# Loading and sorting the second batch's values later in a fused attention and mixture kernel

## The chip, the cores and the metric

The kernel runs on one core of one Trainium2 chip. The metric is the device time of one execution in microseconds (us), as the median of several runs; lower is better. The profile is one execution taken by the hardware profiler. Its engines are PE (TensorE matmul; PEld is its weight load), DVE (VectorE), ACT (ScalarE), POOL (GpSimd) and SP (SyncE, which here only issues DMAs).

## The reference

Four batches of eight heads, 768 positions of 64 numbers each. A small 8 x 8 matrix per head (`sort_net`) is normalised five times over rows and columns, and mixes the eight blocks of 96 positions of keys and values ("sorting"). Each block of queries then attends to the sorted block of the same place. The result, 3072 tokens of 512 numbers, goes through a layer of eight experts, whose outputs are weighted by a matrix P that is balanced in eight rounds.

```python
P = sort_net
for _ in range(5):
    P = exp(P - max(P, -1)); P = P / (sum(P, -1) + 1e-9); P = P / (sum(P, -2) + 1e-9)
k_sorted = einsum('bhij,bhjcd->bhicd', P, k_blocks)
v_sorted = einsum('bhij,bhjcd->bhicd', P, v_blocks)
attn = softmax(q_blocks @ k_sorted.T / 8)
x = (attn @ v_sorted).transpose(0, 2, 1, 3).reshape(3072, 512)
...
for e in range(8):
    out += Pm[:, e:e+1] * (maximum(x @ w1[e], 0) @ w2[e])
```

## The kernel before, in words

The kernel has three phases. In the first, the small matrices are normalised on 32 partitions (lines 413 to 431, ACT and DVE in turn, five rounds) while the first batch's queries, values and keys are loaded; then the whole attention of batch 0 runs with two-bank PSUM tiles called `pair`, four of them. In the second, the attention of batches 1 to 3 is woven, step by step, with the first expert's layer for tokens that are ready (`hidden0` computes its hidden units, `output0` its outputs), with eight one-bank PSUM tiles called `bank`. In the third and by far the longest, from about 115 us, the other experts run with sums in the manner of Strassen. The change touches the first phase and the start of the second.

One batch's attention has these steps. Values: `sort_pair` (two heads at once, line 268) or `sort_values` (line 156) multiply the loaded values by R, the expanded matrix of the batch, and copy the product to the tile `vs`, on ACT (for batch 0 half of them on DVE). `hop` (line 148) then moves `vs` by eight DMAs, one for each block ("piece"), into `vsb`, where the 96 positions of a block lie on partitions; there are two such tiles, one for even and one for odd batches. Keys (k0 to k3, two heads each) are multiplied by R likewise; queries (q0 to q3) are transposed, and ACT copies them to `qTs`. Scores (s0 to s3) are matmuls of both, and ACT takes their exponential into `atp`. A mix (m0 to m3: `wide_mix` in batch 0, `mix` after it) multiplies `atp` by `vsb`, and DVE divides by the sums into `og`: a reciprocal (line 337) and a product (line 339) in batch 0. A turn (t0 to t3) transposes `og`, and ACT or DVE copies it to `xtT`, from which `hidden0` reads; kk numbers its four parts, one for each pair of heads. `logits` (l0, l3) feeds the balance.

The order of the work on PE is written out by hand. The helper `pin` keeps a DMA or an instruction in the program's order on its engine, and almost every matmul is pinned. In the second phase `run_both` takes one step of an attention (or of `sort_values`) and then as many steps of the first expert as a list says; a step of `hidden0` is four matmuls and an activation on ACT (line 372), a step of `output0` four matmuls with w2 (line 379). Every engine works through its own list in order, and waits for others by semaphores; what stands behind a waiting instruction waits as well. PSUM tiles are used in turn, so a matmul can also wait until an engine has read the tile's former content.

The loads from HBM are issued by POOL and form one queue: batch 0's q, v and k first, then a small weight, then batch 1's v (line 97). The loads behind these stand behind a gate (line 454), a tiny copy on POOL that reads the first two pieces of batch 0's `vsb`: w1 in two halves, batch 1's k and q, w2, and then batch 2's v, k and q (line 522). Between the pieces of batch 0 and the gate, POOL also builds batch 1's R (line 453). Pieces: batch 0's are issued by SP, POOL and ACT in turn, batch 1's by SP alone, those of batches 2 and 3 by SP and POOL in turn.

`warm` (line 322) issues matmuls of a zero tile whose product nobody reads; it has `Ibig`, the identity that POOL makes, as its weights. Such unread products stand at the start (four), ahead of `spread` (seven; `spread` expands the normalised matrix, line 437), and here and there in batch 0's attention.

In batch 0's attention the first phase also sorts batch 1's values: `sort_pair(1, ...)` stands between its mixes (line 463), with four copies on ACT, and `hop(1)` at its end (line 476).

Of the kernel before, what the change touches and what calls it, by code (L numbers as in the profile page):

```python
# [25 lines left out]
def kernel(  # L26
# [11 lines left out]
    nc = tc.nc  # L38
# [25 lines left out]
    pin = tc.keep_in_program_order  # L64
    kt, vt, qt = {}, {}, {}

    def load_batch(bb, parts):
        for x, l0, n in parts:
            d, src = {"v": (vt, v), "k": (kt, k), "q": (qt, q)}[x]
            if bb not in d:  # L70
                d[bb] = kvp.tile([128, 8, 384], BF16, name="kvq", bufs=5)
            pin(nc.gpsimd.dma_start(
                out=d[bb][:, l0:l0 + n, :],
                in_=src[bb, l0:l0 + n].rearrange("h (p kk) d -> p h (kk d)", kk=6)))

    w1t = {}
# [15 lines left out]
    Ibig = ones.tile([128, 128], BF16)  # L92
# [1 line left out]
    load_batch(0, [(x, l0, 4) for x in "vk" for l0 in (0, 4)])  # L94
    wg = ones.tile([128, 4, E], BF16)
    pin(nc.gpsimd.dma_start(out=wg, in_=moe_w_gate.rearrange("(kk k) e -> k kk e", k=128)))
    load_batch(1, [("v", 0, 8)])
    blank = perp.tile([128, 512], BF16)
    nc.vector.memset(blank, 0.0)
    mask16 = ones.tile([128, 16], F32)  # L100
# [8 lines left out]
    xtT = xtp.tile([128, 4, N], BF16)  # L109
# [21 lines left out]
    def build_r(bb, eng, n, pbps=None):  # L131

        Rt[bb] = perp.tile([128, 8, 8, 16], BF16, name=f"R{bb % 2}")
        for h in range(0, 8, n):
            ins = eng.tensor_tensor(
                out=mkap(Rt[bb], [Rt[bb].ap[0], [16, 8 * n], [1, 16]] if pbps is None else
                         [Rt[bb].ap[0], [128, n], [16, 8], [1, 16]], off=h * 128),
                in0=(mkap(Pb, [Pb.ap[0], [1, 8 * n], [0, 16]], off=(bb * 8 + h) * 8)
                     if pbps is None else
                     mkap(pbps, [pbps.ap[0], [1, n], [32, 8], [0, 16]], off=h)),  # L140
                in1=mkap(mask16, [mask16.ap[0], [0, 8 * n], [1, 16]] if pbps is None else
                         [mask16.ap[0], [0, n], [0, 8], [1, 16]]),
                op=ALU.mult)
            if eng is nc.gpsimd:
                pin(ins)


    def hop(bb):
        for i in range(NB):
            eng = ((nc.sync, nc.gpsimd, nc.scalar)[i % 3] if bb == 0 else  # L150
                   nc.gpsimd if i % 2 and bb > 1 else nc.sync)
            (pin if bb == 0 else lambda ins: ins)(eng.dma_start(
                out=mkap(vsbt[bb % 2], [[VW, 96], [1, 520]], off=i * 520),
                in_=vs[16 * i:16 * i + 16].rearrange("p kk h d -> p kk (h d)")))
# [98 lines left out]
    held = pp.tile([96, 2], BF16)  # L253
# [67 lines left out]

    def warm(t, n):
        for _ in range(n):
            pin(nc.tensor.matmul(t[:, 0, :], Ibig, blank, start=True, stop=True))

    def wide_mix(hp, pair):
        og[0, hp] = sp.tile([128, NB, 2, 64], BF16, name="og", bufs=2)
        for h in range(2):
            t = pair()
            warm(t, h == 0 and hp > 0)  # L330
            for i in range(NB):
                c, a = (i % 4) * 65, (i * 8 + 2 * hp + h) * 65
                pin(nc.tensor.matmul(t[0:96, i // 4, c:c + 65], at[0, hp, h][0:96, i, :],
                                     vsbt[0][0:96, a:a + 65], start=True, stop=True))
            recips = sp.tile([128, NB], F32, name="recips")
            ps = t[0:96, :, 0:260].rearrange("p b (j x) -> p b j x", j=4)
            nc.vector.reciprocal(out=recips[0:96].rearrange("p (b j) -> p b j", b=2),
                                 in_=ps[:, :, :, 64])
            nc.vector.tensor_mul(
                og[0, hp][0:96, :, h, :].rearrange("p (b j) d -> p b j d", b=2),  # L340
                ps[:, :, :, 0:64],
                mkap(recips, [[recips.ap[0][0], 96], [4, 2], [1, 4], [0, 64]]))
# [21 lines left out]
            yield  # L364

    def hidden0(c0, hTs, hbank, fbs=range(8)):
        for fb in fbs:
            hps = hbank()
            for kk in range(4):
                pin(nc.tensor.matmul(hps[:, 0:384], w1t[0][:, kk, fb * 128:(fb + 1) * 128],  # L370
                                     xtT[:, kk, c0:c0 + 384], start=(kk == 0), stop=(kk == 3)))
            nc.scalar.activation(out=hTs[:, fb, 0:384], in_=hps[:, 0:384], func=AF.Relu)  # L372
            yield

# [31 lines left out]
    with tc.tile_pool(name="ps0", bufs=4, space=bass.MemoryType.PSUM,  # L406
                      reuse_waits="tile") as ps0:
        pair = lambda: ps0.tile([128, 2, 512], F32, name="pair")
        warm(pair(), 4)
        rs = pp.tile([32, 8], F32)  # L410
        cs = pp.tile([32, 8], F32)
        Pt = P.rearrange("p i j -> p j i")
        nc.vector.reduce_max(out=rs, in_=P, axis=AX.X)
        nc.vector.tensor_sub(P, P, mkap(rs, [rs.ap[0], rs.ap[1], [0, 8]]))
        for it in range(5):


            pin(nc.scalar.activation(out=P, in_=P, func=AF.Exp))
            for hp in {2: (0, 1), 3: (2,), 4: (3,)}.get(it, ()):
                wide_queries(hp, pair)  # L420
            if it == 1:
                pin(nc.vector.reduce_sum(out=mask16, in_=Ibig.rearrange("p (j c) -> p c j", c=16),
                                         axis=AX.X))
            pin(nc.vector.reduce_sum(out=rs, in_=P, axis=AX.X))
            nc.vector.reciprocal(out=rs, in_=rs)
            nc.vector.tensor_mul(P, P, mkap(rs, [rs.ap[0], rs.ap[1], [0, 8]]))
            nc.vector.reduce_sum(out=cs, in_=Pt, axis=AX.X)
            if it == 0:
                nc.vector.tensor_scalar_add(cs, cs, 1e-9)
            nc.vector.reciprocal(out=cs, in_=cs)  # L430
            nc.vector.tensor_mul(Pt, Pt, mkap(cs, [cs.ap[0], cs.ap[1], [0, 8]]))

        Prep = perp.tile([32, 8, 8, 16], BF16, name="R1")
        for eng, i0, n in ((nc.vector.tensor_copy, 0, 5), (nc.scalar.copy, 5, 3)):
            eng(Prep[:, i0:i0 + n], mkap(P, [P.ap[0], [8, n], [1, 8], [0, 16]], off=i0 * 8))

        def spread(n):
            t = pair()
            warm(t, n)
            pbps = t[:, 0, 0:256].rearrange("p (i g) -> p i g", i=8)  # L440
            for i in range(8):
                pin(nc.tensor.matmul(pbps[:, i, :], Prep[:, i].rearrange("p j c -> p (j c)"),
                                     Ibig[0:32, 0:32], start=True, stop=True))
            return pbps

        build_r(0, nc.vector, 2, spread(7))
        for hp in range(4):
            sort_pair(0, hp, pair)
        wide_keys(0, pair)
        hop(0)  # L450
        wide_keys(1, pair)
        nc.vector.tensor_copy(Pb, spread(0).rearrange("p i g -> p g i"))
        build_r(1, nc.gpsimd, 4)
        gate = nc.gpsimd.tensor_copy(
            held, mkap(vsbt[0], [[VW, 96], [520, 2]], off=519))
        with tc.issue_after(gate.ins):
            load_w1(0, 0, 512)
            load_w1(0, 512, F)
            load_batch(1, [("k", 0, 8), ("q", 0, 4), ("q", 4, 4)])
            load_w2(0)  # L460
        for x in "s0 k2 s1 k3 s2 s3".split():
            (wide_keys if x[0] == "k" else wide_scores)(int(x[1]), pair)
        for x in "v0 v1 m0 v2 m1 t0 v3 m2 t1 m3 t2 t3".split():
            hp = int(x[1])
            if x[0] == "m":
                wide_mix(hp, pair)
            elif x[0] == "v":
                sort_pair(1, hp, pair)
            else:
                if hp == 3:  # L470
                    warm(pair(), 3)
                turn(0, hp, lambda shape, dt: ps0.tile(
                    [128, 2048], dt, name="pair")[:, 0:768].rearrange(
                        "p (i c) -> p i c", i=NB),
                     nc.vector.tensor_copy if hp == 3 else nc.scalar.copy)
        hop(1)

    def weave(a, b, na, nb):

# [7 lines left out]
    with ExitStack() as c2:  # L487
        pa = c2.enter_context(tc.tile_pool(name="pa", bufs=8, space=bass.MemoryType.PSUM,
                                           reuse_waits="tile"))
        bank1 = lambda shape, dt: pa.tile(shape, dt, name="bank", tag="bank")  # L490
# [20 lines left out]
        def run_both(a, counts):  # L511
            for n in counts:
                next(a, 0)
                run(n)
# [3 lines left out]
        run(8)  # L518
        at1 = attention(1, bank1, "k0 k1 k2 q0 q1 s0 q2 s1 k3 q3 s2 "
                                  "m0 s3 m1,t0 m2,t1 m3 t2 t3,l0 l3")  # L520
        run_both(at1, (1, 1, 1, 1, 0, 1, 0, 1, 0, 0, 1))
        load_batch(2, [(x, 0, 8) for x in "vkq"])
        build_r(2, nc.gpsimd, 4)
        run_both(at1, (1, 2, 1, 2))
# [333 lines left out]
```

## Time and profile before

| | |
|---|---|
| median of 3 runs | 678.94 us (677.23 to 679.38) |
| the profiled execution | 677.66 us |
| its span, first to last instruction | 675.6 us |
| PE, DVE, ACT, POOL busy | 659.3, 542.8, 297.4, 469.5 us |
| end of batch 0's attention (first `hidden0` matmul) | 31.70 us |
| batch 1's v load issued, landed | 7.14, 21.21 us |
| batch 0's pieces: first issue, last landing | 16.34, 23.44 us |
| batch 1's pieces: first issue, last landing | 27.82, 39.8 us |
| first mix of batch 1 (m0) on PE | 50.15 us |
| batch 2's pieces: first issue, last landing | 62.87, 69.35 us |

In a row of the timeline stand the start in us, the time it took, the engine (a q behind it: its sequencer, which issues DMAs), the line of the kernel, the operation, the tile written and the tiles read, the shape, and the number of equal instructions merged into the row. In brackets stands how long the engine had been idle before it, and what released it. Times are from the start of the span.

### The profile page before, as it was taken

What the parts mean: (1) busy time and instruction counts of PE and PEld (TensorE: products, weight loads), DVE (VectorE), ACT (ScalarE), POOL (GpSimd) and SP (SyncE); (2) the same over time, 40 slices, a digit from 0 to 9 for tenths busy, and PEclk for the clock granted to TensorE, in tenths of its full rate; (3) what the DMA queues carried; (4) which work ended last, traced back from release to release, by engine and by line L of the source; (5) the groups of instructions that cost most, each with busy time, mean ns of one, the idle gap of its engine ahead of it and who ended that gap; (6) DMA issues with size and microseconds to landing.
All of it is one profiled execution on the core that took longest, in us unless ns stands there. A gap on an engine that the chain in (4) does not pass through costs nothing.

```text
span 675.6 us, 13268 instructions
## 1 busy us (share of the span) xinstructions
PE 659.3 (98%) x5139; PEld 435.2 (64%) x5139; DVE 542.8 (80%) x1133; ACT 297.4 (44%) x536; POOL 469.5 (69%) x494
## 2 busy tenths in 40 slices
PE   6899999999999999999999999999999999999996
PEld 3566675554666666666666666666666666666675
DVE  7528777673798888888898888888898888888896
ACT  4773863479433334333433333333433343333430
POOL 4702435007987998898897998689886999636745
PEclk9999999999999999999999999999999999999999
DMA  9997964002140340031203040034003120001223
GB/s 157 190 216 115 154 114 63 1 0 41 23 64 2 62 64 1 1 64 20 44 1 62 2 64 0 3 62 63 1 1 65 25 39 1 1 0 64 95 79 141
DMA packets 32735, 36.57 MB, mean 54 GB/s; under 512 B 2016, under 2 KB 25792, under 8 KB 32672
## 3 DMA queue, kind: packets, MB, share of 16 engines
q0 software_dynamic: 26672, 27.32, 25.7%
q1 hardware_dynamic: 5776, 8.20, 3.8%
q8 instruction: 40, 0.66, 0.4%
q10 hardware_dynamic: 224, 0.20, 0.1%
q14 instruction: 23, 0.19, 0.1%
HBM read 52.45 MB, written 6.29 MB: 87 GB/s over the span
## 4 chain that ended last, share of the span: by engine, by line
PE 73%; DVE 1%; POOL 1%; issue 0%; ACT 0%; DVEq 0%
PE oacc L715 36%; PE bk L628 35%; PE bk L715 1%; DVE osbl L680 1%; POOL hs L698 1%; DVE hT L664 0%; DVE hT L667 0%; ACT p L648 0%; DVEq L680 0%
## 5 line engine op out<-in xcount | busy, mean ns | idle before, releaser
L680 DVE SCALAR_TENSOR_TENSOR osbl<-oacc,glog,osbl 128x256 f32<-128x256 f32 (+1 forms) x490 | 255.6, 522 | 61.3 <-PE oacc L715 61.2
L628 PE MATMUL bk<-xtT,w1e 128*128 128x512 bf16 x504 | 149.7, 379 | 0.0
L698 POOL TENSOR_TENSOR hs<-hT 128x512 bf16<-128x512 bf16 (+2 forms) x105 | 99.4, 960 | 67.2 <-DVE hT L667 67.1
L715 PEld LDWEIGHTS <-hs 128*128 128x128 bf16 x1008 | 98.5, 98 | 64.6 <-POOL hs L698 1.5
L715 PEld LDWEIGHTS <-hT 128*128 128x128 bf16 x1008 | 98.6, 98 | 64.5 <-issue 1.3
L670 ACT ACTIVATE hT<-bk 128x512 bf16<-128x512 f32 x84 | 50.3, 598 | 158.8 <-PE bk L628 158.8
L715 PE MATMUL oacc<-w2e,hT 128*128 128x256 bf16 x796 | 119.6, 273 | 0.5 <-ACT hT L670 0.5
L698 POOL TENSOR_TENSOR hs<-hT,hs 128x512 bf16<-128x512 bf16 (+2 forms) x105 | 99.9, 959 | 4.9
L698 POOL TENSOR_TENSOR hs<-hs,hT 128x512 bf16<-128x512 bf16 (+2 forms) x105 | 99.9, 960 | 4.3 <-ACT hT L670 0.4
L628 PE MATMUL bk<-xc,wc 128*128 128x512 bf16 x336 | 99.9, 379 | 0.2 <-ACT p L648 0.2
L715 PE MATMUL oacc<-w2e,hs 128*128 128x256 bf16 x612 | 92.0, 273 | 0.9 <-POOL hs L698 0.9
L656 ACT COPY u<-bk 128x512 f32<-128x512 f32 x84 | 49.3, 586 | 95.2 <-PE bk L628 94.5
L628 PEld LDWEIGHTS <-w1e 128*128 128x128 bf16 x672 | 65.7, 98 | 10.5
L664 DVE CUSTOM_DVE_ANT_0 hT<-bk,p 128x512 bf16<-128x512 f32 x84 | 58.1, 692 | 11.8 <-ACT p L661 6.4
L674 DVE SCALAR_TENSOR_TENSOR h<-bk,hT 128x512 bf16<-128x512 f32 x84 | 57.2, 681 | 5.7 <-ACT hT L670 5.7
L661 ACT COPY p<-bk 128x512 f32<-128x512 f32 x84 | 49.3, 586 | 23.5 <-PE bk L628 23.5
L648 ACT COPY p<-bk 128x512 f32<-128x512 f32 x84 | 49.3, 587 | 20.1 <-PE bk L628 20.1
L652 DVE CUSTOM_DVE_ANT_0 hT<-bk,p 128x512 bf16<-128x512 f32 x84 | 57.2, 681 | 1.1 <-ACT hT L372 0.6
L667 DVE CUSTOM_DVE_ANT_0 hT<-bk,u 128x512 bf16<-128x512 f32 x84 | 57.2, 680 | 1.0 <-PE bk L628 1.0
L715 PE MATMUL oacc<-w2s,hs 128*128 128x256 bf16 x364 | 54.8, 273 | 0.1
L628 PEld LDWEIGHTS <-wc 128*128 128x128 bf16 x504 | 49.3, 98 | 8.0 <-issue 0.4
L628 PE MATMUL bk<-xtT,wc 128*128 128x512 bf16 x168 | 50.0, 379 | 0.0
(138 smaller groups left out, 832.3 us busy)
## 6 DMA issues: line engine op xcount, KB each, us to landing
w2e<-in_moe_w_dram POOLq DMA_DIRECT2D x8, 1024.0 KB, 8.9
w1e<-in_moe_w_dram POOLq DMA_DIRECT2D x7, 1024.0 KB, 8.2
out_dram<-osbl SPq DMA_DIRECT2D x23, 256.0 KB, 2.0
kvq<-in_v_dram POOLq DMA_DIRECT2D x3, 768.0 KB, 14.1
kvq<-in_k_dram POOLq DMA_DIRECT2D x3, 768.0 KB, 13.6
vsb<-vs SPq DMA_DIRECT2D x19, 97.5 KB, 5.3
kvq<-in_q_dram POOLq DMA_DIRECT2D x4, 384.0 KB, 10.6
kvq<-in_q_dram POOLq DMA_DIRECT2D x2, 768.0 KB, 21.9
```

Source lines behind the costliest of these rows:

```text
L628: hold(nc.tensor.matmul(ps, wa[:, kk, :], xa[:, kk, :], start=(first and kk == 0), stop=(kk == 1), skip_group_check=True))
L648: nc.scalar.copy(p1, u)
L652: nc.vector._custom_dve(TENSOR_ADD_SAT, out=c11, in0=w, in1=p1, s0=TOP, s1=0.0)
L656: nc.scalar.copy(u2, u)
L661: nc.scalar.copy(p5, v)
L664: nc.vector._custom_dve(TENSOR_ADD_SAT, out=c22, in0=u, in1=p5, s0=TOP, s1=0.0)
L667: nc.vector._custom_dve(TENSOR_ADD_SAT, out=c12, in0=v, in1=u2, s0=TOP, s1=0.0)
L670: nc.scalar.activation(out=c21, in_=u, func=AF.Relu)
L674: nc.vector.scalar_tensor_tensor(out=h3[e, p][:, i, :], in0=u, scalar=0.0, in1=c22, op0=ALU.max, op1=ALU.subtract)
L680: nc.vector.scalar_tensor_tensor(out=o, in0=ps, scalar=glog[:, t, e:e + 1], in1=o, op0=ALU.mult, op1=ALU.add)
L698: nc.gpsimd.tensor_tensor(out=c, in0=a, in1=b, op=o)
L715: nc.tensor.matmul(ps, h[:, fb, :], w[:, fb, :], start=(first and fb == 0), stop=(fb == 3), skip_group_check=True)
```

## The change

Six edits:

1. Batch 1's v load moves from line 97, ahead of the gate, to the list behind the gate, after batch 1's k and q and ahead of w2.
2. The sorting of batch 1's values leaves batch 0's attention. `sort_values(1, ...)` with `hop(1)` at its end now stands in batch 1's attention, after s0 and ahead of q2. The steps of the first expert are shared out anew; their number up to s2 is the same.
3. Batch 0's pieces are issued by SP and POOL in turn, four each, and no longer by ACT. Batch 1's stay with SP alone.
4. `warm` takes its weights from the zero tile itself. There are eleven unread products at the start instead of four, nine ahead of `spread` instead of seven, three new ones ahead of the third group of queries, and one more in the first mix of batch 0.
5. The mixes and turns of batch 0 keep their order without the value products between them.
6. The first steps of `hidden0` hold three PSUM tiles: for hidden blocks 0, 1 and 2 the products of the first three parts of `xtT` are issued ahead of the first product of the fourth part.

```diff
-    load_batch(1, [("v", 0, 8)])
...
-            eng = ((nc.sync, nc.gpsimd, nc.scalar)[i % 3] if bb == 0 else
-                   nc.gpsimd if i % 2 and bb > 1 else nc.sync)
+            eng = nc.gpsimd if i % 2 and bb != 1 else nc.sync
...
-            pin(nc.tensor.matmul(t[:, 0, :], Ibig, blank, start=True, stop=True))
+            pin(nc.tensor.matmul(t[:, 0, :], blank[:, 0:128], blank, start=True, stop=True))
...
-            warm(t, h == 0 and hp > 0)
+            warm(t, h == 0)
...
     def hidden0(c0, hTs, hbank, fbs=range(8)):
+        held = {}
         for fb in fbs:
-            hps = hbank()
-            for kk in range(4):
-                pin(nc.tensor.matmul(hps[:, 0:384], w1t[0][:, kk, fb * 128:(fb + 1) * 128],
-                                     xtT[:, kk, c0:c0 + 384], start=(kk == 0), stop=(kk == 3)))
+            for f, some in (((0, range(3)), (1, range(3)), (2, range(3)), (0, (3,)))
+                            if (c0, fb) == (0, 0) else
+                            ((fb, (3,) if fb in held else range(4)),)):
+                if f not in held:
+                    held[f] = hbank()
+                for kk in some:
+                    pin(nc.tensor.matmul(held[f][:, 0:384],
+                                         w1t[0][:, kk, f * 128:(f + 1) * 128],
+                                         xtT[:, kk, c0:c0 + 384],
+                                         start=(kk == 0), stop=(kk == 3)))
+            hps = held.pop(fb)
...
-        warm(pair(), 4)
+        warm(pair(), 11)
...
+            if it == 3:
+                warm(pair(), 3)
...
-        build_r(0, nc.vector, 2, spread(7))
+        build_r(0, nc.vector, 2, spread(9))
...
-            load_batch(1, [("k", 0, 8), ("q", 0, 4), ("q", 4, 4)])
+            load_batch(1, [("k", 0, 8), ("q", 0, 4), ("q", 4, 4), ("v", 0, 8)])
...
-        for x in "v0 v1 m0 v2 m1 t0 v3 m2 t1 m3 t2 t3".split():
+        for x in "m0 m1 t0 m2 t1 m3 t2 t3".split():
...
-            elif x[0] == "v":
-                sort_pair(1, hp, pair)
...
-        hop(1)
...
-        run_both(at1, (1, 1, 1, 1, 0, 1, 0, 1, 0, 0, 1))
+        run_both(at1, (1, 1, 1, 1, 0, 1))
+        run_both(sort_values(1, bank1), (0, 0, 1, 0, 0))
+        run_both(at1, (0, 0, 0, 0, 1))
```

## The prediction

> **What bounds the kernel now.** I read the page first: busy shares, then the chain that ended last.
>
> ```profile
> PE 659.3 (98%) x5139; PEld 435.2 (64%) x5139; DVE 542.8 (80%) x1133; ACT 297.4 (44%) x536; POOL 469.5 (69%) x494
> ...
> PE 73%; DVE 1%; POOL 1%; issue 0%; ACT 0%; DVEq 0%
> ```
>
> TensorE is busy for 98% of the span, and the chain is TensorE's own matmuls. So once TensorE has its stream, any microsecond in which it stands still is added to the end. The list of waits from 32 us to the end agrees: TensorE's longest single wait there is 0.9 us and all listed waits sum to about 5 us, so a new delay finds almost nothing to hide in. Next I cut the first part into stretches (busy time of each engine, then granted clock, DMA share, GB/s).
>
> ```profile
> 0.00:12.55 12.55, 7.75 (x59) 3.82 (x59) 8.24 (x37) 5.83 (x11) 6.93 (x14) 1.00 0.96 143
> ...
> 16.00:31.70 15.70, 13.42 (x218) 9.35 (x213) 10.35 (x22) 11.37 (x16) 13.23 (x17) 1.00 1.04 187
> 31.70:50.00 18.30, 18.09 (x236) 11.13 (x236) 4.42 (x9) 13.24 (x28) 0.20 (x1) 1.00 1.27 218
> ```
>
> The change touches two places. Up to 31.7 us (batch 0's attention) TensorE is not the bound: it has 2.3 us of holes in the second row. From 31.7 us it is full (18.09 of 18.30), and there ACT, fourth of the busy columns, has 5 us left, but not evenly. The change moves work from the first place into the second.
>
> **The first stretch: a gain.** What ends it is VectorE's run over the mixes.
>
> ```profile
> 23.75 0.20 DVE L337 RECIPROCAL recips<-pair 96x8 f32<-96x8 f32 x1 [2.69 <-PE pair L333]
> ...
> 29.22 1.26 DVE L339 TENSOR_TENSOR og<-pair,recips 96x512 bf16<-96x512 f32 x2
> 31.09 0.56 DVE L250 COPY xtT<-pair 128x768 bf16<-128x768 bf16 x1 [0.61 <-PE pair L247]
> ```
>
> From 23.75 to 30.48 VectorE has no gap over 0.2 us, so the stretch ends earlier only if this run starts earlier. It starts when batch 0's last sorted piece has landed: the eight pieces are issued from 16.34 and the last lands at 23.44 (SP's third), together with batch 1's v load, which lands at 21.21. The change takes that load out of the way and uses two queues, four pieces each. The nearest row for that is batch 2's pieces, on the same two queues and with no load beside them: first issue 62.87, last landing 69.35, 6.48 us. From 16.34 that gives 22.82, **0.62 us earlier**. ACT's four sorted-value copies (about 3 us) and its two DMA issues (16.34 to 17.87) leave this stretch too. I cost both at nothing: the exponentials they delayed are ready before VectorE needs them, and the cover is VectorE's unbroken run.
>
> The held hidden products then use the 0.65 us in which TensorE waits at 31.70 for VectorE's copy of the last turn. In the changed order the second of the three held banks waits for that same copy, so only three of the nine products come ahead of it: 3 x 0.16 = **0.49 us**. Gain: 1.1 us. Above, it is at most 2.4: the first mix's bank is free only after the fifth exponential (20.84 + 0.81), so VectorE could start no earlier than about 22.0, 1.75 before now, and 0.65 for the wait.
>
> Below, it can be a loss. Unread products cost 2.95/7 = 0.42 us each at 9.60 and (0.82 - 0.39)/2 = 0.21 at 17.68, while the granted clock reads 1.00 in both places; I go by the products. The new ones ahead of the spread (three, and nine for seven) are five more: 2.1 us later if the slow rate still holds then, because the seven now end at 12.55, just ahead of the spread's 12.68. I take nothing: the fast rate came after 4.4 us of unbroken work (8.18 to 12.55), and the eleven products now start at about 1.2 us, as their weights no longer wait for the identity.
>
> **The second stretch: ACT's copies.** Batch 1's eight value products come between the first scores and the second batch of scores. On TensorE they are 8 x 0.163 = 1.3 us. Their eight ACT copies matter more, since ACT has no gap there:
>
> ```profile
> 46.50 0.52 ACT L372 ACTIVATE hTs<-bank 128x384 bf16<-128x384 f32 x1
> 46.87 0.84 ACT L187 COPY qTs<-bank 128x768 bf16<-128x768 bf16 x1
> 47.55 1.69 ACT L226 ACTIVATE atp<-bank 96x384 bf16<-96x384 f32 x4
> 49.04 0.58 ACT L372 ACTIVATE hTs<-bank 128x384 bf16<-128x384 f32 x1
> ```
>
> In the changed order six copies stand behind the hidden activation at 46.50, then the other activation, then two copies. Batch 2's copies run at 0.38 us each (60.39 to 62.28 for five steps). So 46.87 + 6 x 0.38 + 0.37 + 0.38 + 0.53 = 50.4 us for the last copy's end; less 1.1, **49.3 us**.
>
> **The wait that is added.** hop(1) cannot issue before that last copy, and only SP issues it. Before, these eight issues stood at 27.82, 11 us ahead of TensorE's need.
>
> ```profile
> 27.82 5.45 SPq L152 DMA_DIRECT2D vsb<-vs  x8
> ```
>
> The last was issued at 32.59, and the trace has it land after
>
> ```profile
> DMA to landing us min/median/max: 7.2/7.2/7.2
> ```
>
> that is at 39.8, 12.0 us behind the first issue. Loads of the POOL queue ran beside them all the time. They will again: today the queue lands w2 at 47.07 and batch 2's v, k, q at 50.93, 54.81, 58.65, one every 3.9 us. Batch 1's v now stands among them, the w1 load starts about 1 us earlier (its gate is released behind POOL's build of R, some 21.2 instead of 22.1), and batch 2's q waits only for the last value product (behind it on POOL stand batch 2's R and query copies, due at 58.70). The first w2 product, due at about 50.8, still finds w2: with batch 1's v ahead of it, 47.07 + 3.9 - 0.9 = 50.1 at the latest. So I take 12.0: the last piece lands at 49.3 + 12.0 = **61.3 us**. With no load beside it the bound is 4.77 us to the eighth issue and 3.1 to 4.4 to land (batch 2's pieces on SP): 57.2 to 58.5.
>
> Behind the waiting issues on SP stand only batch 2's pieces (62.87 now). Who waits is TensorE, in order.
>
> ```profile
> 48.21 1.03 PE L218 MATMUL bank<-qTs,kTs 64*96 64x96 bf16 x16
> 49.29 1.02 PE L379 MATMUL bank<-w2e,hTs 128*128 128x512 bf16 x4
> 50.15 0.93 PE L236 MATMUL bank<-vsb,atp 96*96 96x65 bf16 x16
> 50.91 1.03 PE L379 MATMUL bank<-w2e,hTs 128*128 128x512 bf16 x4
> ```
>
> The third row is the first mix (m0). Its first eight products each need one piece. Only four scores, queries and keys steps and four w2 products stand between the value products and m0. With banks freed late by ACT, TensorE arrives at m0 at about 52.8 - 1.1 = 51.7 and then stands until 61.3. Behind m0 on its engine are all later matmuls. When the eighth piece is there, nine products of 0.045 us remain: 61.3 + 0.4 = 61.7 for the row that now starts at 50.91. **+10.8 us.** The earlier gain of 1.1 is in it.
>
> **The clock after the wait.** TensorE stands for some 9 us with eight tiny products in between. No row of before shows such a hole, so the cost is bounded: 0 if nothing slows, 4.5 if the slow rate lasts as long as at the start (3.56 to 12.55, 9.0 us at half speed). I take the unbroken 4.4 us ahead of the switch, the nearest to the dense stream that follows here: half of it, **2.2 us**.
> [...]
>
> **Sum.** The profiled execution took 677.66 us (span 675.6, 2.06 around it). 677.66 + 10.8 + 2.2 = **690.7 us**. The median of the three runs is 678.94, 1.28 above it; the range covers this.
>
> **Rivals.**
> - *The pieces land unhindered* (57.2 to 58.5; take 57.9): +7.4, with the clock 687.3, without 685.1. For it: the queue's backlog could be ahead of my reckoning. Against: 8 us of loads are left at 49.3. Chance 0.20.
> - *No slow clock after the wait*, pieces as forecast: 688.5. For it: the little products. Chance 0.20.
> - *The slow rate outlasts the first unread products*: +2.1 ahead of the spread, 692.8. Against: work is less broken than before. Chance 0.07.
> - *The wait is covered*: pieces land before TensorE arrives, and only ACT's delay remains, 52.8 - 1.1 - 50.15 = +1.5: 679.2, no change. Against: TensorE comes 2.4 us behind the first issue, no piece has landed in under 3.1. Chance 0.05.
> - *Faster: the early landing of batch 0's pieces decides.* At its ceiling, 2.4, against 1.3 of value products on TensorE: 676.6 at best. It decides only if TensorE waits under 1.1 us for batch 1's pieces. It would be faster by 1.1, within 0.3%; beyond 0.3% it needs the freed ACT to give yet more. Chance 0.03 in all.
>
> **How the numbers follow.** My forecast, 690.7, has 0.45. 0.3% (2.0 us) is about what a measurement of this kernel can tell from no change. Faster 0.02, same 0.06, slower 0.92. Low end: unhindered landing at its fastest, no slow clock (57.2 + 0.4 - 50.91 = 6.7), 684.3. High end: 10.8 + 4.5 of clock, and the median's 1.28: 694.2; with the gain at nothing, 695.3. Range 684.3 to 695.3.
>
> **What would show it.** In the changed profile: VectorE's first reciprocal near 23.1; the last turn's copy near 30.5; the last vs copy of batch 1 at 49 to 50; eight SP issues behind it over 5 us, each landing after 5 to 7 us; a TensorE row on vsb and atp with gaps of about 9 us in all, released by SP's DMAs; unread-product-like pitch doubled in the w2 products just behind it. It is wrong if TensorE has work in that hole that I do not see, or if the pieces land within 3 us of the last copy.

## The result, and the profile after

| | before | after |
|---|---|---|
| median of 5 runs | 677.92 us (677.22 to 679.38) | 690.40 us (688.77 to 691.32) |
| ratio, 95% interval | | 1.0173 [1.0149, 1.0196] |
| the profiled execution, its span | 677.66, 675.6 | 690.67, 688.9 |

The changed kernel is slower by 1.7%. The profiles show where; times are again from the start of the span.

| us | before | after | forecast |
|---|---|---|---|
| batch 0's pieces: last landing | 23.44 | 23.83 | 22.82 |
| first `hidden0` product | 31.70 | 33.00 | 30.6 |
| last value copy of batch 1 ends | | 52.12 | 49.3 |
| batch 1's pieces: first issue, last landing | 27.82, 39.8 | 52.15, 61.33 | 49.3, 61.3 |
| first w2 product behind m0 | 50.91 | 62.04 | 61.7 |
| first product of m3 | 62.67 | 76.12 | |
| from there to the end | 612.9 | 612.8 | |

The page of the changed kernel: TensorE busy for 9.8 us more, the same chain, and two dents in the granted clock (tenths, each slice 17.2 us).

```profile
PE 669.1 (97%) x5152; PEld 440.0 (64%) x5152; DVE 542.9 (79%) x1133; ACT 297.7 (43%) x540; POOL 469.8 (68%) x495
...
PEclk9896999999999999999999999999999999999999
...
PE 71%; DVE 1%; POOL 1%; issue 0%; ACT 0%; DVEq 0%
```

The stretches in the changed kernel (start:end, length, busy PE, PEld, DVE, ACT, POOL, granted clock, DMA share, GB/s):

```profile
16.00:33.00 17.00, 14.61 (x214) 11.15 (x209) 9.76 (x21) 8.64 (x12) 11.72 (x16) 0.80 0.96 159
33.00:50.00 17.00, 16.74 (x189) 9.85 (x187) 3.94 (x8) 11.47 (x25) 0.20 (x1) 1.00 1.29 205
50.00:63.00 13.00, 8.08 (x80) 4.80 (x80) 2.74 (x9) 6.56 (x16) 4.33 (x5) 0.63 0.98 177
63.00:75.00 12.00, 12.00 (x102) 6.59 (x101) 8.02 (x24) 3.66 (x10) 0.00 (x0) 0.83 0.00 1
```

The same third stretch in the kernel before:

```profile
50.00:63.00 13.00, 13.00 (x134) 7.97 (x133) 9.60 (x32) 6.74 (x17) 1.59 (x2) 1.00 0.74 115
```

The third row of the changed kernel is the new hole: TensorE works 8.08 of 13.00 us, where before it worked all 13.00, and the mean clock of the stretch is 0.63. The first row has a clock of 0.80; before it was 1.00. In the trace of the changed kernel the clock is at half rate from 26.03 to 32.86 and from 53.34 to 66.99, and full otherwise from 5.55 to the last us.

VectorE's run over batch 0's mixes in the changed kernel:

```profile
24.14 0.20 DVE L335 RECIPROCAL recips<-pair 96x8 f32<-96x8 f32 x1 [3.53 <-PE pair L331]
...
28.47 0.20 DVE L335 RECIPROCAL recips<-pair 96x8 f32<-96x8 f32 x1 [0.43 <-PE pair L331]
...
33.20 0.56 DVE L248 COPY xtT<-pair 128x768 bf16<-128x768 bf16 x1 [1.04 <-PE pair L245]
```

It starts 0.39 us later than before, not earlier, and it is no longer unbroken: behind the clock's fall at 26.03 VectorE waits for TensorE's mixes and turns. From the first reciprocal to the start of the last copy it takes 9.06 us; before it took 7.34 (23.75 to 31.09).

The added wait in the changed kernel begins on ACT, with the value copies:

```profile
48.54 2.43 ACT L159 CAST vs<-bank 128x384 bf16<-128x384 f32 x6
50.76 0.59 ACT L378 ACTIVATE hTs<-bank 128x384 bf16<-128x384 f32 x1
51.14 0.98 ACT L159 CAST vs<-bank 128x384 bf16<-128x384 f32 x2
```

SP's queue issues the pieces behind the last of them, which ends at 52.12:

```profile
52.15 5.22 SPq L150 DMA_DIRECT2D vsb<-vs  x8
```

The time from each of these issues to its landing:

```profile
DMA to landing us min/median/max: 4.6/5.9/6.1
```

And TensorE at m0, in its timeline:

```profile
53.63 1.89 PE L385 MATMUL bank<-w2e,hTs 128*128 128x512 bf16 x4
58.14 0.29 PE L234 MATMUL bank<-vsb,atp 96*96 96x65 bf16 x1 [2.62 <-DMA vsb<-vs]
58.85 0.22 PE L234 MATMUL bank<-vsb,atp 96*96 96x65 bf16 x1 [0.42 <-DMA vsb<-vs]
...
60.81 1.42 PE L234 MATMUL bank<-vsb,atp 96*96 96x65 bf16 x12 [0.65 <-DMA vsb<-vs]
62.04 1.90 PE L385 MATMUL bank<-w2e,hTs 128*128 128x512 bf16 x4
```

The last copy ends, SP issues its eight pieces in 5.22 us, each lands 4.6 to 6.1 us later, and TensorE's products of m0 are released by the landings. TensorE is done with the w2 products at 55.52 and the last piece lands at 61.33: 5.81 us, of which TensorE stands idle for 4.4. The w2 products on both sides of the hole take 1.9 us for four; before the change four took 1.03.

### The profile page after: what moved, and what is told of

Its sections match the earlier page's. It is cut to its first block, busy times and chain, and to the rows that moved or that the text cites. A ratio compares the mean times of both kernels' runs of the same rounds, so it can differ in the third digit from the quotient of the medians.

```text
span 688.9 us, 13294 instructions
## 1 busy us (share of the span) xinstructions
PE 669.1 (97%) x5152; PEld 440.0 (64%) x5152; DVE 542.9 (79%) x1133; ACT 297.7 (43%) x540; POOL 469.8 (68%) x495
## 4 chain that ended last, share of the span: by engine, by line
PE 71%; DVE 1%; POOL 1%; issue 0%; ACT 0%; DVEq 0%
PE oacc L722 36%; PE bk L635 35%; PE bk L722 1%; DVE osbl L687 1%; POOL hs L705 1%; DVE hT L671 0%; DVE hT L674 0%; ACT p L655 0%; DVEq L687 0%
## 5 line engine op out<-in xcount | busy, mean ns | idle before, releaser
L635 PEld LDWEIGHTS <-w1e 128*128 128x128 bf16 x672 | 65.7, 98 | 10.5
L668 ACT COPY p<-bk 128x512 f32<-128x512 f32 x84 | 49.3, 587 | 23.2 <-PE bk L635 23.2
L655 ACT COPY p<-bk 128x512 f32<-128x512 f32 x84 | 49.3, 587 | 20.3 <-PE bk L635 20.3
L635 PEld LDWEIGHTS <-wc 128*128 128x128 bf16 x504 | 49.3, 98 | 8.0 <-issue 0.4
## 6 DMA issues: line engine op xcount, KB each, us to landing
vsb<-vs SPq DMA_DIRECT2D x20, 97.5 KB, 4.6
```

What stands on the lines that cost most here:

```text
L635: hold(nc.tensor.matmul(ps, wa[:, kk, :], xa[:, kk, :], start=(first and kk == 0), stop=(kk == 1), skip_group_check=True))
L655: nc.scalar.copy(p1, u)
L668: nc.scalar.copy(p5, v)
```

## The experiments

The theory: the whole loss is the wait of batch 1's m0 for pieces that set off too late, and the half clock around it; the other edits do nothing here. Rivals: the other edits (queues, unread products, held tiles) cost something themselves; the load stream beside the pieces makes most of it; the clock makes most of it. Each ratio below is against the kernel before, run beside it on the same chip, with its 95% interval; e1 to e4 ran together, e5 to e8, and e9 to e11, e12 alone (on the chip of e5 to e8). "Half" is the time in which the granted clock of the profiled execution is at half rate, after its first rise.

**e1: the other edits without the move** (the v load, the value steps, `hop(1)` and the list of `run_both` as before; edits 3, 4, 6 kept).

```diff
+    load_batch(1, [("v", 0, 8)])
...
-        for x in "m0 m1 t0 m2 t1 m3 t2 t3".split():
+        for x in "v0 v1 m0 v2 m1 t0 v3 m2 t1 m3 t2 t3".split():
...
+        hop(1)
...
```

> Edits 3, 4 and 6 alone: batch 1's values are loaded and sorted where they were before. Theory A (the wait of batch 1's first mix for its late pieces carries the loss): no such wait here, so 676 to 678, and the first hidden product 0.5 us earlier than 31.70, by the held products. Theory B (the loss comes from the edits around it: two queues for batch 0's pieces, unread products with other weights): about half of the loss or more stays, 683 and up. Clock by both: full from about 5.6 us on, since the unread products start at 1.2.

Measured: 676.99 us, ratio 0.9988 [0.997, 1.0006]. First hidden product 31.30, no half clock, no wait on `vsb` in m0. With the held tiles it came 0.40 earlier than before, ahead of the last turn's copy (31.50, 0.41 later than before). Without the move the other edits cost nothing in the total.

**e2: the move alone** (the kernel before with edits 1, 2 and 5).

```diff
-    load_batch(1, [("v", 0, 8)])
...
+        run_both(at1, (1, 1, 1, 1, 0, 1))
+        run_both(sort_values(1, bank1), (0, 0, 1, 0, 0))
+        run_both(at1, (0, 0, 0, 0, 1))
```

> Edits 1, 2 and 5 alone, on the kernel before: only the load and the sorting of batch 1's values move. Theory A: 690 to 692, as slow as the whole change or 0.5 us slower, for the held products are missing; the last piece of batch 1 lands near 61 to 62 us. Theory B: 680 or less.

Measured: 689.67 us, ratio 1.0165 [1.0138, 1.0192]; the profiled execution took 687.24. That is just below the 690 to 692 expected; the last piece landed at 59.44 and not at 61 to 62, as the first stretch ended sooner. TensorE in e2:

```profile
50.38 1.02 PE L378 MATMUL bank<-w2e,hTs 128*128 128x512 bf16 x4
54.14 0.23 PE L235 MATMUL bank<-vsb,atp 96*96 96x65 bf16 x1 [2.74 <-DMA vsb<-vs]
...
59.48 0.85 PE L235 MATMUL bank<-vsb,atp 96*96 96x65 bf16 x9 [0.57 <-DMA vsb<-vs]
60.15 1.90 PE L378 MATMUL bank<-w2e,hTs 128*128 128x512 bf16 x4
```

The move alone makes the loss: all eight products wait, 6.5 us in sum. In this execution the clock did not fall in batch 0's attention, and the first hidden product came at 30.13, 1.57 **earlier** than before. So the gain that I forecast for the first stretch exists when the clock stays up; it has two parts, VectorE's run starting 0.94 earlier (22.81 for 23.75) and being 0.63 shorter (6.71 us from the first reciprocal to the last copy, for 7.34). (The other five executions took 688.3 to 691.09, at lower mean clocks.) The last value copy ended 18.74 us behind the first hidden product; the forecast had 18.7.

**e3: sorted sooner** (the changed kernel; batch 1's v is the first load behind w1, and its sorting stands ahead of batch 1's attention, with a step of the first expert beside each of its five).

```diff
-            load_batch(1, [("k", 0, 8), ("q", 0, 4), ("q", 4, 4), ("v", 0, 8)])
+            load_batch(1, [("v", 0, 8), ("k", 0, 8), ("q", 0, 4), ("q", 4, 4)])
...
-        run(8)
+        run(3)
+        run_both(sort_values(1, bank1), (1, 1, 1, 1, 1))
...
-        run_both(at1, (1, 1, 1, 1, 0, 1))
-        run_both(sort_values(1, bank1), (0, 0, 1, 0, 0))
-        run_both(at1, (0, 0, 0, 0, 1))
+        run_both(at1, (1, 1, 1, 1, 0, 1, 0, 1, 0, 0, 1))
```

> The changed kernel with batch 1's values loaded first behind w1 and sorted between the hidden steps ahead of batch 1's keys; the pieces are issued from about 41 us, some 10 us ahead of the first mix. Theory A: no wait for pieces, TensorE stays full; what stays is 1.3 us of value products and the later end of the first stretch (33.0 instead of 31.7): 677.7 + 1.3 + 1.3 = 680.3, 679 to 682. Theory C (ACT, not the pieces, holds up that stretch: eight more copies cost it whatever the place): 684 or more.

Measured: 680.11 us, ratio 1.0024 [1.0007, 1.0041]. TensorE in e3:

```profile
49.89 1.04 PE L385 MATMUL bank<-w2e,hTs 128*128 128x512 bf16 x4
50.77 0.47 PE L234 MATMUL bank<-vsb,atp 96*96 96x65 bf16 x7
51.68 0.55 PE L234 MATMUL bank<-vsb,atp 96*96 96x65 bf16 x9 [0.45 <-DMA vsb<-vs]
52.06 1.03 PE L385 MATMUL bank<-w2e,hTs 128*128 128x512 bf16 x4
```

The pieces set off at 39.57 and took 12.07 us to the last landing, 2.9 longer than in the changed kernel, and still only one wait of 0.45 is left. Same work, same queues: the products, ACT copies and pieces all stand earlier, the pieces by 12.6 us, and some 10 us come back. So the eight copies on ACT in the full stretch are not the loss either. This is the experiment that carries the theory.

**e4: more unread products in batch 0's mixes** (the changed kernel).

```diff
-            warm(t, h == 0)
+            warm(t, (8, 2, 2, 2)[hp] if h == 0 else 0)
```

> The changed kernel with seven more unread products ahead of batch 0's first mix and one more in each of the other three. Theory D (the first stretch ended at 33.0 because its holes let the clock fall at 26.0): clock stays full to the end of the stretch, first hidden product at about 31.0 instead of 33.0, time 688 to 689. Its rival (VectorE and the pieces set that end, the clock only shows the holes): first hidden product at 32.8 to 33.2 and no change, 690 to 691.

Measured: 689.36 us, ratio 1.016 [1.0135, 1.0186]; first hidden product 32.03 and not the 31.0 expected. The clock did stay full across the mixes, but here it had been at half from 13.82 to 17.24, and everything ahead of the mixes came later (last piece 24.81). On the total it is inconclusive. What it does show: with the clock full, VectorE's run over the mixes took 7.10 us, for 9.06 in the changed kernel.

**e5: batch 1's pieces by SP and POOL in turn** (the changed kernel). Batch 2's loads then stand behind the four on POOL, so two things change at once.

```diff
-            eng = nc.gpsimd if i % 2 and bb != 1 else nc.sync
+            eng = nc.gpsimd if i % 2 else nc.sync
```

> The changed kernel with batch 1's pieces on SP and POOL in turn. On POOL they stand ahead of batch 2's loads, which so start only behind them: no load runs beside the pieces and two queues issue them. Theory A with the issue pace as its limit: first issue to last landing falls from 9.2 to about 6.5 us (batch 2's pieces), time down by 2 to 4 us to 686 to 688.5. Rival (what holds the first mix is ACT's late copies, and the landing is covered): no change, 690.

Measured: 688.0 us, ratio 1.0145 [1.0124, 1.0167]. The window shrank to 7.17 us (51.26 to 58.43; about 6.5 expected), and most of the loss stayed.

**e6: 24 unread products of 260 columns ahead of batch 1's m0** (the changed kernel).

```diff
+            for _ in range(24 if (bb, hp, h, b) == (1, 0, 0, 0) else 0):
+                pin(nc.tensor.matmul(ops.rearrange("p a b -> p (a b)"), blank[:, 0:128],
+                                     blank[:, 0:260], start=True, stop=True))
```

> The changed kernel with 24 unread products of 260 columns ahead of batch 1's first mix, in the place where TensorE waits for the pieces. If the slow clock behind the wait costs what the trace shows (14.1 us instead of 11.8 from the end of the first mix to the last one), the clock comes back before the wait ends and the time falls by 1 to 2.3 us, to 688 to 689.5; the wait itself stays. Rival (the clock costs nothing, or the products outlast the wait): 690 to 692.

Measured: 689.5 us, ratio 1.0162 [1.0139, 1.0185]. They ran at full rate in 2.82 us, were over long before the last piece, and the clock fell at 59.14 (53.34 in the changed kernel; without filling also 56.06 in e2 and 59.31 in e10). From w2 to m3 it took 13.67 us (14.08 in the changed kernel). Filling did not avoid the half clock, and whether it delayed it is not shown.

**e7: batch 2's loads behind batch 1's pieces** (the changed kernel; a tiny POOL copy that reads the last two pieces gates the loads).

```diff
-        load_batch(2, [(x, 0, 8) for x in "vkq"])
+        gate2 = nc.gpsimd.tensor_copy(
+            held, mkap(vsbt[1], [[VW, 96], [520, 2]], off=6 * 520 + 519))
+        with tc.issue_after(gate2.ins):
+            load_batch(2, [(x, 0, 8) for x in "vkq"])
```

> The changed kernel with batch 2's loads held until batch 1's last two pieces have landed; the pieces stay with SP alone. Loads as the limit of the landing: first issue to last landing falls from 9.2 to about 8.4 us (4.8 to the eighth issue, 3.1 to 4.4 to land), and the time by about 1 us, to 689. SP's issue pace as the limit: the lag from the last issue falls but the window stays near 9, and the time stays within 1 us of 690.4. Batch 2's loads land near 72 at the latest, before they are needed.

Measured: 688.44 us, ratio 1.015 [1.013, 1.017]. The queues in e7's window, from the first issue to the last landing (packets, MB, share of 16 engines):

```profile
q1 hardware_dynamic: 896, 0.80, 66.2%
```

The landings of its pieces:

```profile
DMA to landing us min/median/max: 2.7/2.8/2.9
```

The queues in the changed kernel's window:

```profile
q0 software_dynamic: 1411, 1.06, 75.1%
q1 hardware_dynamic: 896, 0.80, 32.5%
```

Without a load beside it (no q0 at all) a piece lands in 2.8 us instead of 5.9, and the window is 7.17 us (8.4 or about 9 expected), of which SP's eight issues are 5.06. Yet m0's products still wait, 0.2 to 0.56 us each, and the ratio hardly moves. The w2 products behind m0 come at 60.06, 2 us earlier than in the changed kernel: that is the load stream's part, and the theory that it makes most of the loss has fallen. Late departure alone is enough for 1.5%.

**e8: sorted sooner, in the kernel before** (edits 1, 2, 5 with e3's place for the sorting, and the held tiles; unread products and queues as before).

```diff
...
+            load_batch(1, [("v", 0, 8), ("k", 0, 8), ("q", 0, 4), ("q", 4, 4)])
...
+        run(3)
+        run_both(sort_values(1, bank1), (1, 1, 1, 1, 1))
...
```

> The kernel before with batch 1's values loaded behind the gate, first in the list, and sorted between the hidden steps ahead of batch 1's keys, and with the held products; batch 0's pieces on three queues and the unread products as before. Theory: the move alone ends the first stretch at 30.1 (seen in the profile of the move alone) instead of 31.7, the held products give 0.5, the value products cost 1.3 on TensorE, and no wait for pieces: 677.4 - 1.6 - 0.5 + 1.3 = 676.6, within 0.3% of before, and 3 us under the version with the changed unread products. Rival (the earlier unread products are not to blame there): 679 to 680.5.

Measured: 678.37 us, 1.8 above the 676.6 expected, ratio 1.0019 [1.0002, 1.0036]. The clock stayed full in the profiled execution, so it shows the account of the move without its wait. First hidden product at 30.30, 1.40 earlier than before; from there to m3 33.21 us instead of 30.97, 2.24 more. Of these, 8 value products x 0.163 = 1.31, m0's wait 0.50 and a wait for w2's landing 0.18; 0.25 I can't name. So even placed well, the move pays more in the full stretch (2.24) than it gains in the slack one (1.40). The held tiles gain nothing here: the first hidden product itself waits 0.65 us for the last turn's copy, as before the change.

**e9: the old unread products** (the changed kernel without edit 4) and **e10: three queues for batch 0's pieces** (without edit 3). Both ask what made the clock fall at 26.03.

```diff
-            pin(nc.tensor.matmul(t[:, 0, :], blank[:, 0:128], blank, start=True, stop=True))
+            pin(nc.tensor.matmul(t[:, 0, :], Ibig, blank, start=True, stop=True))
...
-        warm(pair(), 11)
+        warm(pair(), 4)
...
```

> The changed kernel with the unread products as before (edit 4 undone: identity as weights, four at the start, seven ahead of the spread, none new). Theory F (edit 4 makes the first stretch late: its products run out at 11.0, leave a hole to 12.8 and so let the clock fall sooner): clock full through the stretch as in the move alone, first hidden product at 29.6 to 30.5 instead of 33.0, time 687.5 to 688.5. Rival (edit 3 does it: SP's fourth piece lands at 23.8 instead of 22.5 and makes the hole of 1.56 us ahead of the first mix): first hidden product still at 31.9 to 33.1, time near 690.

```diff
-            eng = nc.gpsimd if i % 2 and bb != 1 else nc.sync
+            eng = ((nc.sync, nc.gpsimd, nc.scalar)[i % 3] if bb == 0 else
+                   nc.gpsimd if i % 2 and bb > 1 else nc.sync)
```

> The changed kernel with batch 0's pieces on SP, POOL and ACT as before (edit 3 undone). If edit 3 makes the first stretch late: last piece at 22.5, clock full, first hidden product at 29.6 to 30.5, time 687.5 to 688.5. If edit 4 does it: the clock still falls in the stretch, first hidden product at 31.5 or later, time near 690.

Measured: e9 689.37 us, 1.0147 [1.0112, 1.0181], half from 23.26 to 36.91; e10 688.36 us, 1.0132 [1.0095, 1.0169], half from 25.17 to 35.41. The first hidden products came at 33.05 and 33.62. Undoing either edit alone does not keep the clock up, and e11 below has both undone and its clock falls too: neither is needed for the fall.

**e11: e8 with batch 1's pieces by SP and POOL.**

```diff
             eng = ((nc.sync, nc.gpsimd, nc.scalar)[i % 3] if bb == 0 else
-                   nc.gpsimd if i % 2 and bb > 1 else nc.sync)
+                   nc.gpsimd if i % 2 else nc.sync)
```

> The version with the values sorted sooner and the old unread products, with batch 1's pieces now on SP and POOL, ahead of batch 2's loads. The pieces' window falls from 12.2 us to 7 to 10 and the last 0.6 us of wait at the first mix goes: 677.4 to 678, level with the kernel before. It stays above it if the 1.3 us of value products on a full TensorE cannot be won back by the 1.6 us that the first stretch gains: then 678 to 679.

Measured: 680.07 us (677.4 to 679 expected), ratio 1.0003 [0.9977, 1.003]. The window is 7.18 us, and m0 waits for nothing. But its profiled execution has the clock at half from 25.71 to 35.95 and the first hidden product at 32.79, 2.49 later than e8's, with the same code in the first stretch: VectorE's run over the mixes took 8.80 us, for 6.70 in e8.

**e12: e8 with more unread products in batch 0's mixes.**

```diff
-            warm(t, h == 0 and hp > 0)
+            warm(t, (7, 3, 3, 3)[hp] if h == 0 else 0)
```

> The version with the values sorted sooner and the old unread products (678.37 us; its executions lie at 677.8 to 678.4 and at 681 to 683), with seven unread products ahead of batch 0's first mix and three ahead of each other one, about as much TensorE work as the value products that have left the stretch. If their absence lets the clock fall in the upper executions, these become rare and the median stays at 678: no execution or one in twelve above 680. Rival (the clock falls for other reasons, or the products get in the mixes' way): a third of the executions stay above 680, or all are 0.5 us and more slower.

Measured: 678.69 us, ratio 1.0013 [1.0004, 1.0022]. Full clock, first hidden product at 31.31, one us behind e8's profile, and its fastest execution 0.7 us behind e8's (678.46 for 677.76): the filling has a price. What it changes is TensorE's share in the first stretch. That stretch in e8:

```profile
16.00:30.30 14.30, 11.80 (x210) 8.78 (x207) 10.07 (x22) 8.63 (x12) 11.33 (x15) 1.00 0.86 151
```

The same in e12:

```profile
16.00:31.31 15.31, 14.00 (x225) 9.79 (x220) 9.69 (x21) 8.60 (x12) 11.35 (x15) 1.00 0.83 140
```

TensorE is busy for 82.5% and 91.4% of it; the kernel before had 85.5%. Each run also has the mean granted clock of each execution. One spell of half clock like that from 26.03 to 32.86 in the changed kernel, 6.83 us, lowers it by 3.41/676 = 0.005, so by this estimate 0.995 or less means as much half clock as one such spell or more:

| | executions at 0.995 or less | kernel before, run beside it |
|---|---|---|
| e1 (value products in the first stretch) | 1 of 12 | 2 of 23 |
| e3, e8, e11 (products gone) | 8 of 12, 4 of 12, 8 of 12 | 2 of 23, 1 of 17, 6 of 17 |
| e12 (products gone, filled) | 0 of 11 | 0 of 15 |

The table says how often the clock falls, not where. With the products gone it falls more often than in the kernel before beside it, and with unread ones in their place not once. But the kernel before did not fall beside e12 either, so that the filling keeps the clock up is a hint and not shown.

No kernel tried is faster than the one before beyond its interval; e1 comes nearest, at 0.9988.

## Why the prediction was right, and where it was wrong inside

**The total** came out as forecast (690.7 against 690.67 in the profiled execution and a median of 690.40). That close an agreement is luck: two errors of its steps, of 2.8 us each, cancelled, a later start of batch 1's pieces and a shorter window for them. The mechanism, m0's wait for late pieces, is not luck.

- *What bounds the kernel: right.* Behind m3 the two profiles differ by 0.1 us in 613: nothing of a delay is given back.
- *The first stretch, forecast as a gain of 1.1: this step failed.* It became a loss: the first hidden product, which no longer waits for the last copy, came 1.30 later than before, the first one behind that copy 2.11 (33.81 for 31.70). Two terms of it fell. The pieces landed at 23.83, not 22.82. In e9, on the same two queues, they did land at 22.82, in e4 at 24.81, and in e2, on three, at 22.5, so this term moves by a us or more from kernel to kernel; why is open (SP's fourth issue took 1.12 us here and 1.14 in e9). And I had taken the eight value products out of TensorE without asking what they did for its clock: it fell at 26.03, and VectorE's run grew by 1.72 us. That this run has a fixed length, so that only an earlier start helps, was the wrong reading behind it. It took 7.34 us before, 6.7 in e2, e3 and e8 (products gone, clock full), 7.39 in e12 (unread products in their place, ACT's copies still gone) and 8.6 to 9.3 in the seven profiles with the clock at half in it. So without the value products it is 0.6 shorter, which I had put at nothing, and with the clock at half 1.9 to 2.6 longer than that. The held products gave what was forecast here: the wait of 0.65 ahead of them is 0.16, 0.49 less; in e8, e9 and e11 the 0.65 is still there. e2 and e8, where the clock stayed up and the pieces landed at 22.5 and 22.67, show a gain of 1.57 and 1.40; e11, with e8's code in this stretch but the clock at half, shows a loss of 1.09.
- *ACT's eight copies: right.* 19.12 us from the first hidden product to the last copy's end, 18.74 in e2, 18.7 forecast. The end itself came 2.8 later than forecast: 2.4 from the first stretch and 0.4 here.
- *The pieces' window of 12.0 us: the size was wrong.* It took 9.18. The mechanism was right, as the windows with their MB of loads beside the pieces show: none 7.2 (e7), 1.06 MB 9.2 (changed kernel), 1.60 MB 10.5 (e2), 1.84 MB 12.0 (before). I took the row from the middle of the load stream; at 52.15 less of that stream was left, and its last load landed at 60.57. The end, 61.33, met the forecast of 61.3 only because the late start and the short window are both 2.8 us.
- *TensorE's wait: right in kind*, and shown: e2 has it and loses 1.65%, e1 lacks it and loses nothing, and in e3, e8 and e11 it goes with the earlier sorting and the loss goes too, up to 0.2%. The hole itself was forecast too long, 9.6 us from TensorE's arrival at 51.7 to the last piece at 61.3. It was 8.04 in e2 (51.40 to 59.44), by the shorter window, and 5.81 in the changed kernel, where TensorE came only at 55.52, late from the first stretch and from w2 products at half rate. That cost nothing in the sum, since the last landing and not the arrival sets the end.
- *The clock behind the wait: right in size* (from w2 to m3 14.08 us, 11.76 before, 2.32 more; 2.2 forecast; 11.77 in e3 and e8), *wrong in its place.* It had fallen at 53.34, ahead of the wait, and rose at 66.99, 5 us behind it; in e2 and e7 it fell inside the wait (56.06, 56.84). The price follows the time at half rate: in all eight kernels with the wait, half of the time from the first w2 product behind m0 to the clock's rise is 1.37 (e2) to 2.67 us (e9), and from w2 to m3 they take 1.22 to 2.51 more than before, always about 0.15 less than that half. So the rival that the clock makes most of the loss has fallen: e2 pays 1.22 for it and loses 1.65%.

Of the rivals, the unhindered landing is e7's: even then 1.5% is lost. No kernel with the wait kept its clock; its price was least in e2 (12.98 us from w2 to m3). The slow rate at the start did not outlast the first unread products: in the changed kernel the clock rose at 5.55 (eleven of them took 4.68 us from 1.20 on, three at 7.19 took 0.82), in the one before at 12.2. The covered wait came true only where the sorting was moved. The early landing of batch 0's pieces did not decide: e2 has it (22.5) and loses 1.65%.

What stays open is what decides, in one execution, whether the clock falls in batch 0's attention: kernels with the same stretch (e8 and e11) differ in it, and so do executions of one kernel.

## What to carry to other kernels

Work that is taken out of a stretch with slack and put into a full one is paid for there (e8: 2.24 us, for 1.40 gained), and the move's price is that of its whole chain (copies, eight issues on one queue, landings) against the first consumer that works in order. Sort when the data has landed, not just ahead of its use; here that took the loss away and made no gain (ratio 1.0024 in e3, 1.0019 in e8). And before work is taken from TensorE, ask whether it keeps its clock up: with the products gone 20 of 36 executions (e3, e8, e11) had a mean clock of 0.995 or less, for 9 of 57 of the kernel before beside them.

## What the runs showed of the hardware

- **The clock's changes lay on a grid in the profile of the changed kernel:** they are 6, 2, 6 and 4 steps of 3.413 us apart (5.55, 26.03, 32.86, 53.34, 66.99). TensorE was at work ahead of both falls: in the 3.41 us ahead of 26.03 it was busy for 1.77, in those ahead of 53.34 for 2.85, with small products. Behind the fall at 26.03 it had no idle time at all for 6.83 us, two steps, before the clock rose at 32.86. What decides a fall is not shown.
- **Most of the spread between executions goes with the clock.** Over 72 executions of the kernel before, a mean clock lower by 0.005 goes with 2.5 us more, and a straight line through them leaves 0.12 of the variance (the 37 at 1.000 take 677.5 us on average, the four at 0.990 take 682.6).
- **One queue issued a piece of 97.5 KB every 0.61 to 0.65 us (e7)**, so eight pieces from SP needed 7.2 us even with nothing beside them, 4.45 to the eighth issue and 2.7 to its landing; by two queues they needed 7.2 beside 1.14 MB of loads (e11).
